# Exponentials and the feed-forward product g split in place in PSUM, a new share-out of the splits among engines, and norms from a matmul with ones

## The chip, the cores and the metric

The kernel runs on one core of a Trainium2 chip. The metric is the device time of one execution in microseconds; lower is better. Times are given in us unless marked ns.

## The reference

Three layers follow each other, all in float32, for B = 2 batches, H = 8 heads, S = 768 tokens of D = 64.

```python
q_n = q / (norm(q) + 1e-6)          # also k_n, c_n
q_assign = argmax(einsum('bhsd,hcd->bhsc', q_n, c_n))   # 16 clusters; k_assign alike
scores = where(q_assign == k_assign, q @ k.T / 8, -1e9)
attn = exp(scores - max(scores)); attn /= sum(attn) + 1e-9
x = (attn @ v)                      # 1536 tokens x 512
h = x @ w_in; g = h * clip(h + 3, 0, 6) / 6; x = g @ w_out           # 512 -> 2048 -> 512
out = sum_e p_e * (relu(x @ w1[e]) @ w2[e])                          # 4 experts, 512 -> 1024 -> 512
```

## The kernel before

**Stages.** For each batch there is an attention, a first feed-forward stage (class Moe1) and a second one (class Moe2). They run in the order attention 0, Moe1(0), Moe2(0) with attention 1 worked in beside it, Moe1(1), Moe2(1). Attention 0 has nothing beside it but the first four of 32 weight tiles to be converted. Moe1(0) carries the other 28 conversions (`conv_w`: float64 bit patterns to float32, four VectorE instructions L770 to L775 a tile, then a split, L749 on ScalarE and L750 on GpSimd). They can start only when the memory of attention 0 is free, since their pools open when its pools close.

**High and low parts.** To keep float32 accuracy each operand is split into a rounded high part and a low remainder, and three matmuls take the place of one (`mm3`, L789 to L791). So each product needs a copy with rounding (the high part, mostly ScalarE) and a subtraction (the low part, VectorE or GpSimd).

**A unit of attention** is 128 queries of one head against all 768 keys; a batch has 48. `scores` puts the score into a tile of two PSUM banks (a ring of three tiles in batch 0, of two in batch 1; a dummy matmul L708 stands ahead in batch 0), VectorE takes the row maximum (L717), ScalarE the exponential with its sum into an SBUF tile e (L718), VectorE scales and inverts the sum (`sums`, L726 and L727). `halves` then makes the two float16 halves p of the probabilities, in one of three ways named by a letter: "P" is GpSimd scaling e in place (L732), ScalarE rounding (L733), GpSimd subtracting (L734); "A" is ScalarE rounding with the scale (L737) and VectorE subtracting (L741); "D" is GpSimd rounding (L739) and VectorE subtracting (L741). In batch 0 the 48 units are 22 P, 13 A and 13 D; in batch 1 they are 12 P and 36 D. A DMA transpose (L673) turns p into pt, matmuls (L686) multiply it with the values, and L694 and L696 split the result.

**Preparation of a pair of heads** (`prep`, four pairs a batch) loads q and k transposed, splits them (L520 to L530, L538), multiplies them with the centroids (L554), transposes these scores (L562), divides them by the norms and makes the one-hot rows of the clusters, which are appended to q and k as rows of the mask. The norms come from a second copy of q and k in natural layout (tensor nat, two loads a pair): `norms` squares it on ScalarE (L495), sums it on VectorE (L496); the root is taken by ScalarE in batch 0 (L505, `roots`) and by GpSimd as a power in batch 1 (L500).

**Moe1** takes its product into a PSUM bank of a ring of three, shared with Moe2 and with the preparation of batch 1. `g1` makes t (L820 on ScalarE, L821 on VectorE, into SBUF), g's high part from t on ScalarE (L822) and its low part on GpSimd (L824) in batch 0, except for every fourth, and on VectorE (L826) otherwise.

**Order.** A class `Order` collects all instructions with what they read and write, and emits them in the order in which a model of the engines would start them; ties go by priorities, planned times that come from the settings `PAR`. Each engine runs its queue in that order.

Of the kernel before, what the change touches and what calls it, by code (L numbers as in the profile page):

```python
# [9 lines left out]
F32 = mybir.dt.float32  # L10
# [10 lines left out]
NEG = 2.0 ** 100  # what a key of another cluster loses; absorbs any score in float32  # L21
PSC = 1024.0  # scale of the probabilities in float16
VSC = 16384.0  # scale of the values in float16, on top of the largest sum over a partition of their head


def _f32(u):
# [3 lines left out]
# Bounds of a float64's high word (seen as float32) whose value float32 can hold.  # L30
# [5 lines left out]
# Settings of the plan: pool depths, the order's look-ahead, priorities in microseconds.  # L36
# [43 lines left out]
class Pool:  # L80
    """A ring of tile slots; opened with its group."""
# [8 lines left out]
class Group:  # L90
    """Pools that open together, once the groups in `after` are closed."""
# [8 lines left out]
class Buf:  # L100
    """A tile that its first writer allocates."""
# [230 lines left out]
def body(ctx: ExitStack, tc: tile.TileContext, qk, nat, vd, cent, w_in, w_out, probs, w1, w2, out):  # L332
# [679 lines left out]
```

## Time and profile before

| | us |
|---|---|
| runs | 1087.26, 1088.27, 1088.45 (median 1088.27) |
| profiled execution, span from first to last instruction | 1088.1 |
| TensorE matmul busy in it | 995.6 (91%) |
| VectorE busy | 634.4 (58%) |
| ScalarE busy | 478.7 (44%) |
| GpSimd busy | 497.8 (46%) |

For the profiled execution nothing but its span is listed; the median of the runs is 0.2 us above that span. A busy share over the whole span says little here, since the stages have different limits; the rows further down are taken by stage. In a row of a group the mean of one instruction stands behind its total, and behind the second bar the time in which its engine sat idle just before such instructions, with what ended it.

### The profile page before, as it was taken

The page shows a single profiled execution, that of the slowest core. Times are in us where ns is not written, and L with a number is a line of the kernel's source. Part 1 is how long each engine was busy: PE and PEld are TensorE (multiplying, and loading weights), DVE is VectorE, ACT ScalarE, POOL GpSimd, SP SyncE. Part 2 cuts the span into 40 slices and gives each one's busy share as a digit, 9 for nine tenths or more (in the row PEclk, how much of TensorE's full clock was granted, in tenths as well). Part 3 has the DMA queues.
Part 4 walks back from the last instruction along what each step waited for, and adds up shares of the span by engine and source line. Part 5 has one row for each costly group of instructions (what it writes and reads, how often), then busy time and mean ns, then how long its engine had stood idle before and what let it go on. Part 6 is the DMA issues. An engine that isn't in the chain of part 4 may idle for free.

```text
span 1088.1 us, 15473 instructions
## 1 busy us (share of the span) xinstructions
PE 995.6 (91%) x5699; PEld 898.5 (83%) x5699; DVE 634.4 (58%) x1103; ACT 478.7 (44%) x893; POOL 497.8 (46%) x385
## 2 busy tenths in 40 slices
PE   3666677988999999999999999999999999999998
PEld 1555556887898888888898898999999899999997
DVE  8999995999536785576476475334453222222222
ACT  6667774545255554345345343444342232222220
POOL 3576864546346776356256164234332333132330
PEclk9678888999999999999999999999999999999999
DMA  8599799676006486367266176222121221112211
GB/s 259 128 201 184 140 187 242 223 245 200 30 2 208 125 168 148 94 134 162 80 145 137 44 156 155 77 78 79 41 67 48 78 78 64 53 50 69 78 39 58
DMA packets 192363, 129.32 MB, mean 119 GB/s; under 512 B 155488, under 2 KB 155488, under 8 KB 192288
## 3 DMA queue, kind: packets, MB, share of 16 engines
q1 hardware_dynamic: 192288, 128.34, 46.1%
q8 instruction: 44, 0.72, 0.3%
q14 instruction: 31, 0.25, 0.1%
HBM read 74.51 MB, written 11.53 MB: 79 GB/s over the span
## 4 chain that ended last, share of the span: by engine, by line
PE 45%; DVE 18%; issue 16%; DMA 9%; POOL 8%; ACT 3%; SPq 1%; POOLq 0%; ACTq 0%; DVEq 0%
PE psm L789 12%; PE psm L791 12%; PE psm L790 12%; DMA pt<-p 6%; POOL w L750 4%; DVE p L741 4%; DVE ut L717 2%; PE psg L790 2%; DVE wconv L773 2%; DVE wconv L770 2%; PE psv L686 2%; PE psg L789 2%; PE psg L791 2%; DVE wconv L775 1%; POOL p L734 1%
## 5 line engine op out<-in xcount | busy, mean ns | idle before, releaser
L750 POOL TENSOR_TENSOR w<-wraw,w 128x512 fp32r<-128x512 f32 x160 | 213.6, 1365 | 289.7 <-ACT w L749 283.6
L864 ACT ACTIVATE h<-psm 128x384 fp32r<-128x384 f32 x128 | 62.4, 488 | 254.9 <-PE psm L791 252.1
L789 PE MATMUL psm<-x2h,w 128*128 128x384 f32 x512 | 173.2, 338 | 0.0
L791 PE MATMUL psm<-x2h,w 128*128 128x384 f32 x512 | 171.8, 336 | 0.0
L790 PE MATMUL psm<-x2l,w 128*128 128x384 f32 x512 | 171.5, 335 | 0.0
L865 DVE SCALAR_TENSOR_TENSOR h<-psm,h 128x384 fp32r<-128x384 f32 x128 | 71.0, 555 | 144.9 <-ACT h L864 144.7
L789 PE MATMUL psm<-w,h 128*128 128x512 f32 x384 | 151.5, 395 | 0.4 <-DVE h L865 0.4
L791 PE MATMUL psm<-w,h 128*128 128x512 f32 x384 | 150.8, 393 | 0.0
L790 PE MATMUL psm<-w,h 128*128 128x512 f32 x384 | 150.4, 392 | 0.0
L880 DVE SCALAR_TENSOR_TENSOR oa<-psm,pr,oa 128x512 f32<-128x512 f32 x84 | 62.8, 748 | 100.8 <-PE psm L791 100.8
L718 ACT ACTIVATE e<-pss,ut 128x768 f32<-128x768 f32 x96 | 86.0, 897 | 72.4 <-DVE ut L717 50.3
L789 PEld LDWEIGHTS psm<-x2h,w 128*128 128x128 f32 x512 | 96.1, 188 | 4.1 <-issue 2.4
L749 ACT ACTIVATE w<-wraw 128x512 fp32r<-128x512 f32 x160 | 93.7, 624 | 11.8 <-PE psm L791 8.1
L741 DVE SCALAR_TENSOR_TENSOR p<-e,ut,p 128x768 f16<-128x768 f32 x62 | 87.6, 1420 | 17.5 <-POOL p L739 15.7
L790 PEld LDWEIGHTS psm<-x2l,w 128*128 128x128 f32 x512 | 96.2, 188 | 1.3
L791 PEld LDWEIGHTS psm<-x2h,w 128*128 128x128 f32 x512 | 96.1, 188 | 0.0
L790 PE MATMUL psg<-g,w 128*128 128x384 f32 x256 | 88.9, 347 | 6.2 <-DVE g L826 4.4
L789 PE MATMUL psg<-x1h,w 128*128 128x384 f32 x256 | 87.3, 341 | 7.7 <-DVE t L821 7.6
L717 DVE TENSOR_REDUCE ut<-pss 128x1 f32<-128x768 f32 x96 | 90.0, 944 | 4.6 <-PE pss L712 4.5
L789 PE MATMUL psg<-g,w 128*128 128x384 f32 x256 | 87.9, 343 | 4.9 <-DVE t L821 4.5
L791 PE MATMUL psg<-g,w 128*128 128x384 f32 x256 | 87.4, 341 | 0.3 <-POOL w L750 0.3
L791 PE MATMUL psg<-x1h,w 128*128 128x384 f32 x256 | 86.7, 339 | 0.0
(125 smaller groups left out, 1913.4 us busy)
## 6 DMA issues: line engine op xcount, KB each, us to landing
wraw<-in_w SPq DMA_DIRECT2D x128, 256.0 KB, 3.2
r<-in_w_in SPq DMA_DIRECT2D x16, 512.0 KB, 5.0
r<-in_w_out SPq DMA_DIRECT2D x16, 512.0 KB, 4.4
nat<-in_nat SPq DMA_DIRECT2D x16, 384.0 KB, 4.4
raw<-in_qk SPq DMA_DIRECT2D x16, 384.0 KB, 4.2
scr_i<-wconv SPq DMA_DIRECT2D x16, 256.0 KB, 2.4
scr_o<-wconv SPq DMA_DIRECT2D x16, 256.0 KB, 3.2
wraw<-scr_i SPq DMA_DIRECT2D x16, 256.0 KB, 2.6
```

What stands on the lines that cost most here:

```text
L686: nc.tensor.matmul(ps[64 * q:64 * q + 64], vs[vi][:, q, t], pts[q][:, :, pi * NT + t], start=i == 0, stop=i == n - 1)
L717: dve(S, p, lambda: nc.vector.tensor_reduce(out=nb(), in_=ps[:, :, 0:HS], axis=AX.XY, op=ALU.max, negate=True), [ps], [(tb, n)])
L718: act(S, p, lambda: nc.scalar.activation(out=e.t.rearrange("p (a b) -> p a b", a=2), in_=ps[:, :, 0:HS], func=AF.Exp, bias=nb(), scale=1.0 ...
L741: dve(S, p, lambda: nc.vector.scalar_tensor_tensor(out=pp[:, j, 1], in0=e.t, scalar=rs(), in1=pp[:, j, 0], op0=ALU.mult, op1=ALU.subtract) ...
L749: act(512, p, lambda: nc.scalar.activation(out=w[:, 0], in_=raw.t, func=AF.Copy), [raw], [(w, 0)])
L750: pool(512, p, lambda: nc.gpsimd.tensor_tensor(out=w[:, 1], in0=raw.t, in1=w[:, 0].bitcast(F32), op=ALU.subtract), [raw, (w, 0)], [(w, 1)])
L789: nc.tensor.matmul(o_, ah, bh, start=i == 0, stop=False)
L790: nc.tensor.matmul(o_, ah, bl, start=False, stop=False)
L791: nc.tensor.matmul(o_, al, bh, start=False, stop=i == 3)
L864: act(MB, p, lambda: nc.scalar.activation(out=h[:, 0], in_=ps[:, 0:MB], func=AF.Relu), [ps], [(h, 0)], ps=True)
L865: dve(MB, p, lambda: nc.vector.scalar_tensor_tensor(out=h[:, 1], in0=ps[:, 0:MB], scalar=0.0, in1=h[:, 0].bitcast(F32), op0=ALU.max, op1=A ...
L880: dve(512, p, lambda: nc.vector.scalar_tensor_tensor(out=oa[:, t], in0=ps.t, scalar=q, in1=oa[:, t], op0=ALU.mult, op1=ALU.add), [ps, pr], ...
```

## The change

The score tile is no longer copied into SBUF: a new letter "M" writes the exponential over the scores in PSUM, and both ScalarE's rounding and VectorE's subtraction read it there. In batch 0 the units become 31 M, 16 P and 1 A, in batch 1 24 D, 12 M and 12 P. In `g1` the product t is written over its PSUM tile, and g's two parts are made from there, the low one always on VectorE. The tensor nat and its loads are gone, with `norms` and `roots`: ScalarE squares the transposed q and k, a matmul with a matrix of ones per head sums them over the 64 rows, and the result goes the way of the centroid scores (copy by ScalarE, three transposes); the root is a power on GpSimd (two instructions of 12 columns a pair), for the first pair of batch 0 a root on ScalarE. The centroid scores leave the ring of score tiles for the ring of single banks (one bank in batch 0). The model in `Order` learns that GpSimd's instructions and VectorE's with two SBUF operands exclude each other (`lock`), and counts 10.8 ns more for a matmul. The settings are other ones; the pool e goes from 6 to 4 tiles, sm from 2 to 3, and the pair order's last two entries are exchanged.

```diff
-    ka=["APDPPDPDADPA", "PADPPAPAAPAP", "PPDPPDDAAPAA", "PDPDPDPDPPAD"],
-    kb="DDDP",
+    ka=["MMPMMPMMPMMP", "MMPMMPMMPMMP", "MMPMMPMMPMMA", "MMPMMPMMPMMP"],
+    kb="DMPD",
...
-                dma(393e3, p, lambda nt=nt, i=i: nc.sync.dma_start(out=nt.t, in_=nat[b, hp, :, 12 * i:12 * i + 12]), [], [nt])
-                act(S, p, lambda nt=nt: nc.scalar.activation(out=nt.t, in_=nt.t, func=AF.Square), [], [nt])
-                dve(S, p, lambda nt=nt, sl=sl: nc.vector.tensor_reduce(out=self.n2[:, sl], in_=nt.t, axis=AX.X, op=ALU.add), [nt], [key])
...
+            for q in range(2):
+                act(S, p(G["sqx"]), lambda q=q: nc.scalar.activation(out=sq[q].t, in_=raws[q].t, func=AF.Square), [raws[q]], [sq[q]])
+            for which in range(2):
+                ps = Buf(p_pm[b], [128, 512], F32, "psc", "prep")
+                def cmm(ps=ps, which=which):
+                    for q in range(2):
+                        lhs, rhs = (ct[:, 2 * hp + q], raws[q]) if which else (bones.t, sq[q])
+                        for f in range(2):
+                            r0 = 64 * f + 32 * q
+                            nc.tensor.matmul(ps[r0:r0 + 32, 0:HS], lhs, rhs[:, f * HS:f * HS + HS], start=True, stop=True)
...
+                act(24, p(4), lambda: nc.scalar.activation(out=fac.t, in_=nsq(), func=AF.Sqrt), [tr[0]], [fac], ps=True, tab=AF.Sqrt)
+            else:
+                dve(24, p(4), lambda: nc.vector.tensor_copy(out=fac.t, in_=nsq()), [tr[0]], [fac])
+                for j in range(2):
+                    pool(12, p(4), lambda js=js: nc.gpsimd.tensor_tensor(out=fac[:, js], in0=fac[:, js], in1=half[:, 0:12], op=ALU.pow), [], [fac], ns=180.0)
...
+            if kind == "M":
+                e, ev = ps, src
+            else:
+                e = self.buf("e", [128, 2, HS], F32)
...
-                if kind == "A":
+                if kind in "AM":
...
-            dve(MB, p, lambda: nc.vector.scalar_tensor_tensor(out=t.t, in0=t.t, scalar=1.0, in1=ps[:, 0:MB], op0=ALU.min, op1=ALU.mult), [ps], [t])
-            act(MB, p, lambda: nc.scalar.activation(out=g[:, 0], in_=t.t, func=AF.Copy), [t], [(g, 0)])
-            if b == 0 and f != 3:
-                pool(MB, p, lambda: nc.gpsimd.tensor_tensor(out=g[:, 1], in0=t.t, in1=g[:, 0].bitcast(F32), op=ALU.subtract), [t, (g, 0)], [(g, 1)])
+            dve(MB, p, lambda: nc.vector.scalar_tensor_tensor(out=ps[:, 0:MB], in0=t.t, scalar=1.0, in1=ps[:, 0:MB], op0=ALU.min, op1=ALU.mult), [t], [ps])
+            act(MB, p, lambda: nc.scalar.activation(out=g[:, 0], in_=ps[:, 0:MB], func=AF.Copy), [ps], [(g, 0)], ps=True)
+            dve(MB, p, lambda: nc.vector.tensor_tensor(out=g[:, 1], in0=ps[:, 0:MB], in1=g[:, 0].bitcast(F32), op=ALU.subtract), [ps, (g, 0)], [(g, 1)])
```

## Rows read from the trace of the kernel before

**Rows 1.** By stretch: length, busy PE, PEld, DVE, ACT, POOL; TensorE clock, DMA share, GB/s

```profile
0.00:30.00 30.00, 12.76 (x62) 7.21 (x62) 26.61 (x65) 20.89 (x31) 10.17 (x13) 1.00 0.80 260
30.00:120.00 90.00, 58.57 (x388) 46.19 (x389) 88.97 (x166) 65.09 (x119) 65.99 (x47) 0.77 0.81 161
120.00:172.00 52.00, 38.32 (x312) 31.19 (x307) 43.31 (x87) 34.41 (x66) 33.89 (x25) 0.84 0.94 171
172.00:285.00 113.00, 96.32 (x510) 89.07 (x508) 100.19 (x151) 52.27 (x97) 54.95 (x37) 0.92 0.67 214
285.00:700.00 415.00, 407.31 (x2428) 367.93 (x2428) 247.27 (x437) 190.11 (x363) 217.94 (x176) 1.00 0.50 120
700.00:1088.10 388.10, 382.31 (x2012) 356.90 (x2011) 128.04 (x198) 115.97 (x219) 114.88 (x88) 1.00 0.20 62
```

**Rows 2.** Groups by line, VectorE in 0 to 172 us (attention 0)

```profile
L717 DVE TENSOR_REDUCE ut<-pss 128x1 f32<-128x768 f32 x48 | 44.9, 941 | 0.9 <-PE pss L712 0.8
...
L741 DVE SCALAR_TENSOR_TENSOR p<-e,ut,p 128x768 f16<-128x768 f32 x25 | 38.9, 1567 | 2.1 <-ACT p L737 1.7 <-POOL p L739 0.4
...
L526 DVE SCALAR_TENSOR_TENSOR qa<-raw,qa 64x768 fp32r<-64x768 f32 x8 | 11.3, 1416 | 0.3
...
L496 DVE TENSOR_REDUCE n<-nat 128x12 f32<-128x768 f32 x8 | 7.5, 945 | 0.2
```

**Rows 3.** The same view, GpSimd, ScalarE and TensorE in 0 to 172 us

```profile
L718 ACT ACTIVATE e<-pss,ut 128x768 f32<-128x768 f32 x48 | 42.8, 893 | 18.5 <-DVE ut L717 15.8 <-DVE sv L641 2.0 <-DVE ut L726 0.5
...
L734 POOL TENSOR_TENSOR p<-e,p 128x768 f16<-128x768 f32 x22 | 39.9, 1820 | 6.6 <-ACT p L733 6.3
...
L732 POOL TENSOR_SCALAR e<-e,ut 128x768 f32<-128x768 f32 x22 | 24.5, 1114 | 23.7 <-DVE ut L726 9.9 <-ACT e L718 5.9 <-DVE ut L727 4.0
...
L708 PE MATMUL pss<-junk,ident_b 128*128 128x384 bf16 x48 | 19.5, 407 | 33.4 <-ACT e L718 33.4
...
L739 POOL TENSOR_SCALAR p<-e,ut 128x768 f16<-128x768 f32 x12 | 12.1, 1011 | 3.1 <-DMA pt<-p 1.6 <-issue 1.1 <-DVE tv L633 0.2
L737 ACT ACTIVATE p<-e,ut 128x768 f16<-128x768 f32 x13 | 12.1, 932 | 4.4 <-DMA pt<-p 3.0 <-DVE ut L727 1.1 <-ACT e L718 0.2
```

**Rows 4.** Timeline, 54 to 58 us: start, duration, engine, line

```profile
54.58 1.95 POOL L734 TENSOR_TENSOR p<-e,p 128x768 f16<-128x768 f32 x1
54.96 2.38 DVE L741 SCALAR_TENSOR_TENSOR p<-e,ut,p 128x768 f16<-128x768 f32 x1
```

**Rows 5.** All instructions of line 865: ns minimum, median, maximum, times

```profile
L865 DVE SCALAR_TENSOR_TENSOR h<-psm,h x128: 532/558/558, 334.3 to 1076.5; 128x384 fp32r<-128x384 f32 x128
```

**Rows 6.** Groups by line, VectorE and GpSimd in 172 to 285 us (Moe1 of batch 0)

```profile
L750 POOL TENSOR_TENSOR w<-wconv,w 128x512 fp32r<-128x512 f32 x20 | 34.7, 1753 | 13.1 <-ACT w L749 9.0 <-issue 4.1
...
L775 DVE SCALAR_TENSOR_TENSOR wconv<-r,wconv 128x512 int32<-128x512 int32 x28 | 24.9, 890 | 0.2
L773 DVE SCALAR_TENSOR_TENSOR wconv<-r,wconv 128x512 int32<-128x512 int32 x28 | 23.6, 842 | 0.2
L824 POOL TENSOR_TENSOR g<-t,g 128x384 fp32r<-128x384 f32 x16 | 19.9, 1241 | 38.4 <-ACT g L822 29.5 <-PE psg L791 8.9
L770 DVE TENSOR_SCALAR wconv<-wconv 128x512 f32<-128x512 f32 x28 | 19.0, 680 | 1.8 <-ACT wconv L769 1.8
...
L826 DVE TENSOR_TENSOR g<-t,g 128x384 fp32r<-128x384 f32 x5 | 4.9, 980 | 0.6 <-ACT g L822 0.6
```

**Rows 7.** All instructions of line 770

```profile
L770 DVE TENSOR_SCALAR wconv<-wconv x32: 412/420/1515, 20.2 to 273.8; 128x512 f32<-128x512 f32 x32
```

**Rows 8.** All instructions of line 773

```profile
L773 DVE SCALAR_TENSOR_TENSOR wconv<-r,wconv x32: 677/684/1664, 48.9 to 278.0; 128x512 int32<-128x512 int32 x32
```

**Rows 9.** Groups by line, 331 to 700 us (Moe2 of batch 0 beside attention 1)

```profile
L500 POOL TENSOR_TENSOR n<-n,half 128x6 f32<-128x6 f32 x16 | 24.3, 1524 | 11.5 <-DVE n L496 7.4 <-DVE n L570 2.0 <-DVE ut L726 1.3
...
L554 PE MATMUL psc<-raw,ct 128*32 128x384 f32 x32 | 3.4, 498 | 0.0
...
L562 PE MATMUL psct<-ident,sc 128*128 128x128 f32 x12 | 2.0, 272 | 0.0
```

More of the change, by code (lines that the diff above doesn't have):

```diff
@@ L143, in group, with add @@
         return g
-    def add(self, eng, dur, prio, fn, reads=(), writes=(), dma=0.0, cols=0, tab=None):
+    def add(self, eng, dur, prio, fn, reads=(), writes=(), dma=0.0, cols=0, tab=None, lock=False):
         t = Task()
+        t.lock = lock or eng == "POOL"
         t.cols, t.tab = cols, tab
@@ L244, in plan @@
                     s = t.ready if t.ready > fe else fe
+                    if t.lock and port > s:
+                        s = port
                     ok = True
@@ L295, in plan @@
                 free[t.eng] = end
+                if t.lock:
+                    port = end
             t.end = end
@@ L331, in body @@
 @with_exitstack
-def body(ctx: ExitStack, tc: tile.TileContext, qk, nat, vd, cent, w_in, w_out, probs, w1, w2, out):
+def body(ctx: ExitStack, tc: tile.TileContext, qk, vd, cent, w_in, w_out, probs, w1, w2, out):
     nc = tc.nc
@@ L424, in body @@
     ct = fixed([128, H, 32], F32, "ct")
+    bones = fixed([128, 32], F32, "bones")
     cn = fixed([128, D], F32, "cn")
@@ new lines, in prep, with ctr @@
+            tr = []
+            for which in range(2):
[6 more added lines that the diff above has]
+                            nc.tensor.matmul(ps[r0:r0 + 32, 0:HS], lhs, rhs[:, f * HS:f * HS + HS], start=True, stop=True)
+                px = p(G["psx"] + 0.5 * which)
+                pe(0.7, px, cmm, [*raws, ct] if which else [*sq, bones], [ps], 4 * HS)
+                sc = self.buf("sc", [128, HS], F32)
+                act(HS, px, lambda sc=sc, ps=ps: nc.scalar.activation(out=sc.t, in_=ps[:, 0:HS], func=AF.Copy), [ps], [sc], ps=True)
+                ps = Buf(p_pm[b], [128, 512], F32, "psct", "prep")
+                def ctr(ps=ps, sc=sc):
+                    for i in range(3):
+                        nc.tensor.transpose(ps[:, i * 128:i * 128 + 128], sc[:, i * 128:(i + 1) * 128], ident.t)
+                pe(0.33, p(G["psx"] + 0.3 + 0.5 * which), ctr, [sc], [ps])
+                tr.append(ps)
@@ L663, in block @@
                     tb = self.buf("tiny", [128, 8], F32, "ut")
-                    es = [self.scores(qa, qb, ka, kb, blk * BQ + (j0 + n) * 128, tb, n, p(q * JQ + j0 + n)) for n in range(step)]
+                    es = [self.scores(qa, qb, ka, kb, blk * BQ + (j0 + n) * 128, tb, n, p(q * JQ + j0 + n), kinds[(q * JQ + j0 + n) % len(kinds)]) for n in range(step)]
                     self.sums(tb, step, p(q * JQ + j0))
@@ L893, in body @@
     centroids(-50.0)
-    for hp in range(NP):
-        a0.norms(hp, G["nat0"] if hp == 0 else 4.0 + 0.5 * hp, 0)
-    a0.roots(0, 1, -49.7)
-    a0.roots(1, NP, G["nroot"])
     when = {(x // NBQ, x % NBQ): T_A + i * 2 * JQ * T_UNIT for i, x in enumerate(G["seq"])}
```

165 lines of the change are left out of this document (68 added, 97 removed).

## The prediction

> **What bounds the kernel now.** I read the busy times by stretch first [rows 1]. They show three regimes. From 285 us on TensorE has work all the time: it is busy for 407.3 of 415 us up to 700 and for 382.3 of 388.1 after that, at full clock. Whatever moves work among the other engines there can win at most the 13.5 us that are left, and work added to TensorE lengthens the run. From 0 to 172 us (attention 0) VectorE is busy for 26.6 + 89.0 + 43.3 = 158.9 us, in the middle stretch for 89.0 of 90, while TensorE, ScalarE and GpSimd have room (TensorE 58.6, ScalarE 65.1, GpSimd 66.0 of 90). From 172 to 285 us (Moe1 of batch 0 with the weight conversions) VectorE is busy again, for 100.2 of 113 us, and TensorE loses 16.7 us there. So VectorE sets the first 285 us, and what is saved on it there brings the long TensorE part forward.
>
> Second, I read the groups by line of attention 0, to see what VectorE's time is made of [rows 2]. L741, the low part of p, takes 1567 ns on average, while the reduction of as many columns L717 takes 941. The timeline shows why [rows 4]: L741 starts at 54.96 while GpSimd's subtraction L734 runs from 54.58 to 56.53, and ends at 57.34, 0.81 us after GpSimd is done. Two operands in SBUF make VectorE wait for a running GpSimd instruction, and that time counts as busy. An instruction with one operand in PSUM does not show it: L865 runs 128 times beside GpSimd's weight splits and never takes more than 558 ns [rows 5].
>
> **The change part by part.** The sum is made against the span of 1088.1 us; the median of the runs lies 0.2 us above it.
>
> *Norms, batch 0.* The eight sums L496 go: 8 x 945 ns = 7.5 us off VectorE [rows 2]. All of them are in the stretch that VectorE bounds, so they count in full. What comes for them on VectorE is three copies of 24 columns, under half a us together. GpSimd gets six roots of 12 columns. A root of 6 columns takes 1524 ns in batch 1 [rows 9]; one of 12 costs between that and twice that, six between 9 and 18 us, and I take 13.5. ScalarE squares as often as before. The matmul with ones and its transposes lie in a stretch where TensorE has a third of its time free [rows 1].
>
> *Probabilities, batch 0.* The 25 L741 of this stretch cost 38.9 us [rows 2]. After it there are 31 of kind M and one of kind A. For M, which reads PSUM, the bound from below is the reduction L717 from PSUM over the same 768 columns, 0.94 us, that from above twice L865, which has half the columns, 1.12 us [rows 2, 5]. I take 1.0: 31 x 1.0 + 1.57 = 32.6 us, a gain of 6.3 us (8.2 and 2.6 at the bounds).
>
> The Trainium skill speaks against this: its page VectorE: DVE Perf Modes, section "The TRN2 errata — SBUF-src ops pay a fixed extra latency per instruction", gives VectorE a fixed 120 cycles for a source in PSUM and 58 for one in SBUF. By it each M would take 62 cycles more, an estimated 65 ns at that page's 0.96 GHz, 2.0 us in all, and the result would be 1078. The trace doesn't show such a price: the reduction of 768 columns takes 941 ns from PSUM (L717) and 945 from SBUF (L496) [rows 2].
>
> *GpSimd, batch 0.* A unit of kind P costs it 1.114 + 1.820 = 2.93 us, one of kind D 1.01 [rows 3]. 22 P and 12 D make 76.5 us, 16 P make 46.9; with the roots GpSimd falls from 110 us in this stretch to 94, by 15%. VectorE's other instructions with two SBUF operands are blocked less: L526 alone runs 8 x (1.416 - 0.945) = 3.8 us over the one-operand time [rows 2]. The gain lies between 0 and that 3.8 as a whole; I take 2, since L526 is not the only one.
>
> *ScalarE, batch 0.* Roundings go from 35 (22 P, 13 A) to 48, so 13 x 0.93 = 12 us more, on 120 us before [rows 1, 3]. In some 158 us that is 84%: hidden beside VectorE. The exponential now writes PSUM, for which no row has a price; it reads PSUM already at 893 ns [rows 3], and the rounding from SBUF takes 932, so I take no difference, and up to 0.04 x 31 = 1.2 us either way on an engine with room.
>
> *The ring of score tiles.* An M unit keeps its tile through the rounding (0.93 us) and the low part (1.0), at least 1.9 us longer. 31 units make 59 us, over three tiles 20 us. From below it is nothing, if TensorE runs that far ahead: it sits idle for 33.4 us before L708 until an exponential has freed a tile [rows 3], and VectorE's queue, not the tile, is what these tiles are waiting in. VectorE would need about 145 us for 48 units, 3.0 a unit, and three tiles give each unit 9 us, so I take 2 us of the 20.
>
> Attention 0: -7.5 - 6.3 - 2 + 2 = -13.8 us.
>
> *Moe1, batch 0.* The 28 conversions in 172 to 285 us are blocked by GpSimd: L770 takes 680 ns against a median of 420, L773 842 against 684, L775 890 [rows 6 to 8]. With L771 taken like L770 and L775's floor like L773's, that is 28 x (2 x 0.26 + 0.158 + 0.206) = 24.8 us. L824 is 19.9 of GpSimd's 55.0 us there and goes; 36% of the blocking is 9.0 us. Against it VectorE gets these 16 subtractions, at L865's 0.558 us [rows 5], 8.9 us, and the five L826 fall from 0.980 to 0.558, -2.1 us. Net -2.2 us, between +6.8 (nothing relieved) and -18 (all of it).
>
> *Batch 1.* TensorE gets a second set of L554 and L562, 3.4 + 2.0 = 5.4 us at most [rows 9], in a stretch where it has 7.7 of 415 us free [rows 1]. Some of it falls into such a gap; I take +4 (0 to 5.4). Twelve units M for D and the missing L496 relieve VectorE, which sets nothing there (247 of 415 us); the missing loads of nat relieve the DMA queue, whose share is 0.50. In the last stage g's parts come from PSUM beside a VectorE at a third of its time: 0.
>
> Sum: 1088.1 - 13.8 - 2.2 + 4 = 1076.1, as a median 1076.
>
> **The rivals.** *The blocking goes altogether.* With M at its lower bound (-1.9), no price for the score tiles (-2), L526 at its floor (-1.8) and no blocking in the conversions (-15.8) it is 1054.6. For it: the blocking is a matter of who runs beside whom, and of GpSimd's subtractions six of 22 L734 leave and all L824 [rows 3, 6]. Against: the weight splits L750 stay, and they are 34.7 of its 55 us in Moe1 [rows 6]. Chance 0.18.
>
> *The transposes set attention 0.* The DMA share is 0.81 from 30 to 120 us and 0.94 after that [rows 1], 122 us of work in 142. If it can't be packed closer, only the 7.5 us of L496, most of which come ahead of the first transpose, are won there: 1088.1 - 7.5 - 2.2 + 4 = 1082.4. For it: 0.94 in the last stretch. Against: L739 and L737 wait only 1.6 and 3.0 us for a transpose [rows 3]. Chance 0.14.
>
> *The score tiles set attention 0: slower.* If all three tiles are booked all the time, the 20 us appear in full in place of the 2: 1076.1 + 18 = 1094. It decides from 16 us on; below that the run is still no slower than before by more than 0.2%. For it: the 33.4 us in which TensorE already waits for a free tile [rows 3], and each M passes VectorE three times. Against: VectorE's 89 of 90 us, which make that wait back-pressure. The Trainium skill's page ScalarE: Activation LUTs, section "Step-by-step: what each stage is for", recommends PSUM as ScalarE's destination only where TensorE does not need most of it; it does here, and that caveat is this rival. No run so far shows which holds. Chance 0.12.
>
> *The product banks set Moe1: no change.* g's rounding and subtraction keep a bank at least 2 x 0.56 us longer. 32 such tiles over a ring of three make 12 us, if the banks are booked all the time, and with 5.4 instead of 4 us in batch 1 it is 1089. For it: TensorE loses 16.7 us in that stretch, VectorE's queue is full and is now passed twice. Against: twelve matmuls fill a bank, and 510 of them take 113 us there [rows 1], so that a bank is needed every 2.7 us and three give each 8. Chance 0.10.
>
> **How the numbers follow.** The forecast has 0.46; its own range is 1066 to 1086. Faster by over 0.2% (2.2 us, about what a measurement of this kernel can tell from no change) is nearly all of it (0.45), the first rival (0.18), 0.13 of the second and 0.01 of the last: 0.77. Within 0.2% lie 0.05 of the last rival and 0.01 each of forecast and second: 0.07. Slower: the third (0.12) and 0.04 of the last: 0.16. The range from 1054 to 1094 leaves out half of the first and of the third rival, 0.15.
>
> **What the profile would show.** Right: the mean of L741's successors with a PSUM operand at 1.0 us, all within 0.1; VectorE still over 90% busy until attention 0 ends, and that end, now about 172, near 158; the first product of Moe1 as much earlier; the conversions' four lines shorter in sum by some 9 us; TensorE at full clock from then on with 4 us more of small matmuls in batch 1. Wrong: VectorE idle between units while TensorE waits for a tile (the score ring), a DMA share near 1 with waits for p's tiles (the transposes), TensorE waiting for the low part of g (the banks), or an M split that takes as long as before.

## The result, and the profile after

The kernel after takes 1097.37 us (median of 4 runs, 1096.75 to 1101.66) against 1088.35 for the kernel before beside it: ratio 1.0084, 95% interval 1.0061 to 1.0108. It is slower by 0.8%, where the prediction said 1076 and faster. The profiled execution is the one of 1101.66 us, some 4 us above the other three; its span is 1099.9. One count given with the change is wrong: its settings make 32 M, 15 P and 1 A of batch 0's 48 units, not 31, 16 and 1. The splits of one M and of the A come after 172 us.

The busy times by stretch, as in [rows 1], of the kernel after:

```profile
0.00:30.00 30.00, 15.56 (x85) 7.85 (x85) 24.82 (x75) 23.28 (x40) 12.12 (x15) 1.00 0.57 179
30.00:120.00 90.00, 61.17 (x398) 44.23 (x399) 69.67 (x144) 65.74 (x113) 51.31 (x36) 0.75 0.81 156
120.00:172.00 52.00, 38.17 (x275) 29.70 (x273) 45.26 (x104) 39.82 (x75) 18.56 (x14) 0.84 0.84 158
172.00:285.00 113.00, 101.91 (x595) 98.82 (x596) 92.82 (x163) 57.68 (x108) 29.60 (x22) 0.95 0.69 211
285.00:700.00 415.00, 400.70 (x2340) 345.48 (x2340) 243.81 (x440) 193.46 (x362) 187.83 (x145) 0.99 0.46 112
```

VectorE did lose its work: 24.82 + 69.67 + 45.26 = 139.8 us up to 172 us, 19.1 less than before [rows 1]. But attention 0 is not shorter. VectorE is now busy for 69.67 of the 90 us in the middle, where it was busy for 89; the time saved turned into idle time.

To see where the span went I cut each trace at four events: the first score matmul, the first product of Moe1(0), the first of Moe2(0), and the point where 55% of the recorded products are done, which is after attention 1. Between them lie these times in us, for all later kernels too; each ratio is to runs of the kernel before made beside that kernel. The medians are of all runs, the stretches of the one profiled execution:

| kernel | median | ratio, 95% | start | attention 0 | Moe1(0) | Moe2(0) with attention 1 | rest |
|---|---|---|---|---|---|---|---|
| before | 1088.4 | | 25.9 | 139.5 | 166.1 | 388.4 | 368.2 |
| after | 1097.4 | 1.0084 [1.0061, 1.0108] | 23.9 | 142.7 | 156.6 | 410.8 | 365.8 |
| e1 | 1090.4 | 1.0016 [0.9998, 1.0034] | 23.5 | 141.6 | 156.4 | 401.1 | 365.8 |
| e2 | 1113.8 | 1.0235 [1.0213, 1.0257] | 23.7 | 154.0 | 160.0 | 407.3 | 365.8 |
| e3 | 1103.6 | 1.0131 [1.0108, 1.0155] | 23.9 | 151.9 | 158.2 | 402.1 | 365.8 |
| e4 | 1086.9 | 0.9976 [0.9965, 0.9988] | 26.3 | 136.8 | 165.4 | 389.5 | 365.9 |
| e5 | 1097.5 | 1.0080 [1.0051, 1.0109] | 28.6 | 144.5 | 162.5 | 392.0 | 365.9 |
| e6 | 1108.3 | 1.0168 [1.0144, 1.0192] | 22.6 | 154.1 | 160.7 | 402.5 | 368.2 |
| e7 | 1107.2 | 1.0162 [1.0144, 1.0180] | 29.0 | 141.8 | 166.9 | 397.4 | 368.2 |
| e8 | 1095.1 | 1.0056 [1.0032, 1.0081] | 26.3 | 147.7 | 165.5 | 387.9 | 365.9 |
| e9 | 1092.0 | 1.0023 [1.0008, 1.0038] | 24.9 | 139.4 | 168.8 | 387.9 | 368.3 |
| e10 | 1093.0 | 1.0040 [1.0028, 1.0052] | 24.7 | 138.8 | 167.6 | 390.4 | 368.2 |
| e11 | 1097.8 | 1.0079 [1.0054, 1.0103] | 26.5 | 139.6 | 164.8 | 397.8 | 368.2 |
| e12 | 1089.6 | 1.0008 [0.9996, 1.0019] | 24.1 | 141.0 | 155.9 | 400.7 | 365.8 |
| e13 | 1102.1 | 1.0118 [1.0096, 1.0141] | 28.4 | 145.2 | 169.9 | 389.0 | 368.2 |
| e14 | 1122.2 | 1.0313 [1.0274, 1.0351] | 25.6 | 161.9 | 158.9 | 410.2 | 365.8 |
| e15 | 1088.4 | 0.9986 [0.9971, 1.0001] | 24.2 | 142.8 | 153.0 | 401.9 | 365.8 |
| e16 | 1108.5 | 1.0178 [1.0155, 1.0202] | 27.1 | 153.4 | 168.8 | 390.4 | 368.2 |
| e17 | 1081.3 | 0.9940 [0.9918, 0.9961] | 23.3 | 142.3 | 155.4 | 393.1 | 365.8 |
| e18 | 1101.9 | 1.0127 [1.0101, 1.0154] | 24.1 | 154.5 | 161.8 | 393.4 | 365.8 |

So before to after: start -2.0, attention 0 +3.2, Moe1(0) -9.5, Moe2(0) with attention 1 +22.4, rest -2.4. Together that is 11.7 us, where the medians differ by 9.0: some 3 us of it belong to the two executions and not to the kernels. Two places call for a reason: attention 0, which should have got 13.8 us shorter, and Moe2 with attention 1, which should have got 4 us longer.

The chain of work that ended last, share of the span by engine, in the kernel before and in the kernel after:

```profile
PE 45%; DVE 18%; issue 16%; DMA 9%; POOL 8%; ACT 3%; SPq 1%; POOLq 0%; ACTq 0%; DVEq 0%
```

```profile
PE 58%; DMA 11%; issue 7%; DVE 7%; ACT 5%; POOL 4%; SPq 1%; ACTq 0%; POOLq 0%; DVEq 0%
```

"issue" is time in which the engine waited for nothing that the profile shows. The shares of VectorE, GpSimd and issue fell; what they gave up went to TensorE and, less, to DMAs and ScalarE.

**Attention 0.** The line numbers have moved: L724 is L717 of before, L749 L741, L725 L718, L710 L708, L513 L526; L570 are the new roots. The groups of 0 to 172 us that answer to [rows 2, 3], VectorE, ScalarE, TensorE, GpSimd:

```profile
L724 DVE TENSOR_REDUCE ut<-pss 128x1 f32<-128x768 f32 x48 | 44.7, 949 | 11.5 <-PE pss L714 11.3
...
L749 DVE SCALAR_TENSOR_TENSOR p<-pss,ut,p 128x768 f16<-128x768 f32 x31 | 31.2, 1014 | 7.5 <-ACT p L745 7.0 <-issue 0.2
...
L725 ACT ACTIVATE pss<-pss,ut 128x768 f32<-128x768 f32 x32 | 27.8, 868 | 10.6 <-DVE ut L724 10.2 <-DVE ut L732 0.3
...
L710 PE MATMUL pss<-junk,ident_b 128*128 128x384 bf16 x48 | 18.5, 384 | 21.8 <-DVE p L749 15.1 <-ACT e L725 3.2 <-DVE ut L732 2.0
...
L725 ACT ACTIVATE e<-pss,ut 128x768 f32<-128x768 f32 x16 | 14.3, 897 | 2.6 <-DVE ut L724 2.6
L570 POOL TENSOR_TENSOR fac<-fac,half 128x12 f32<-128x12 f32 x6 | 14.1, 2351 | 9.7 <-DVE fac L567 9.6
...
L513 DVE SCALAR_TENSOR_TENSOR qa<-raw,qa 64x768 fp32r<-64x768 f32 x8 | 9.7, 1224 | 0.6 <-ACT qa L507 0.5
```

VectorE now waits 11.3 us for scores and 7.0 for ScalarE's rounding (L745), where it waited 0.8 for scores before [rows 2]. TensorE's wait ahead of a score has another releaser: 33.4 us for an exponential before [rows 3], now 15.1 for the low part L749 of an M unit, which gives the tile back. One such wait in the order of TensorE's queue, from the timeline of 94 to 102 us (start, duration, wait in brackets):

```profile
95.91 0.34 PE L710 MATMUL pss<-junk,ident_b 128*128 128x384 bf16 x1
...
96.88 0.85 PE L547 MATMUL psc<-sq,bones 128*32 128x384 f32 x8
101.44 0.34 PE L710 MATMUL pss<-junk,ident_b 128*128 128x384 bf16 x1 [3.70 <-DVE p L749]
```

From one score to the next pass 5.5 us, 3.70 of them idle. But in all TensorE waits less for tiles than before (21.8 us ahead of L710 in the row above, 33.4 in [rows 3]), and it waits somewhat more for transposes. The largest waits for either in 26 to 165 us (total, times, longest), first before, then after:

```profile
PE pss L708 <- ACT e L718: 33.4, 20, 5.0
PE psv L686 <- DMA pt<-p: 4.2, 2, 2.6
```

```profile
PE pss L710 <- DVE p L749: 15.1, 9, 3.7
PE psv L688 <- DMA pt<-p: 6.7, 5, 2.7
```

The price of the M split itself is what was predicted; the 31 that fall ahead of 172 us (minimum, median, maximum):

```profile
L749 DVE SCALAR_TENSOR_TENSOR p<-pss,ut,p x31: 1007/1017/1019, 31.0 to 170.6; 128x768 f16<-128x768 f32 x31
```

**Moe2 with attention 1.** The waits of TensorE there, 323 to 712 us (total, times, longest):

```profile
PE pss L712 <- ACT e L725: 8.4, 6, 2.0
PE psv L688 <- DMA pt<-p: 3.4, 4, 1.1
PE psm L797 <- ACT h L869: 1.3, 1, 1.3
```

The first row is waits for a score tile. In the kernel before, the same view of 323 to 712 us has none; its longest entry is

```profile
PE psv L686 <- DMA pt<-p: 6.2, 7, 1.9
```

The granted clock is below 1.00 in two places of the stretch. One lies behind a wait for a score tile (1.93 us, ending at 477), the other behind a wait of a product of Moe2 for its h (L797, ending at 339). By stretch:

```profile
330.00:340.00 10.00, 8.65 (x45) 7.47 (x43) 4.90 (x6) 6.89 (x11) 4.97 (x4) 1.00 0.78 243
340.00:350.00 10.00, 9.71 (x40) 6.78 (x41) 6.05 (x15) 2.35 (x7) 0.25 (x1) 0.83 0.03 5
350.00:360.00 10.00, 10.00 (x60) 8.60 (x60) 4.15 (x8) 4.79 (x9) 7.53 (x5) 1.00 0.40 131
...
470.00:480.00 10.00, 8.07 (x37) 7.04 (x36) 5.83 (x10) 3.59 (x7) 2.51 (x2) 0.88 0.37 80
480.00:490.00 10.00, 8.95 (x63) 6.46 (x62) 6.47 (x11) 4.53 (x8) 2.59 (x3) 0.95 0.52 115
...
650.00:660.00 10.00, 8.03 (x46) 7.71 (x45) 5.94 (x14) 6.31 (x13) 7.30 (x6) 1.00 0.64 169
660.00:670.00 10.00, 10.00 (x74) 8.11 (x73) 6.81 (x13) 5.39 (x10) 3.47 (x3) 1.00 0.70 158
```

In either place a part was at 1.2 GHz and not at 2.4; by the granted clock that is 1.7 us of work each, some 3.4 of the 22.4. The other five waits for a tile have no lower clock behind them, as the rows of 650 to 670 us show for the longest (1.97 us).

### The profile page after: what moved, and what is told of

Its sections match the earlier page's. It is cut to its first block, busy times and chain, and to the rows that moved or that the text cites. A ratio compares the mean times of both kernels' runs of the same rounds, so it can differ in the third digit from the quotient of the medians.

```text
span 1099.9 us, 15658 instructions
## 1 busy us (share of the span) xinstructions
PE 1013.4 (92%) x5787; PEld 898.2 (82%) x5787; DVE 600.9 (55%) x1128; ACT 501.2 (46%) x925; POOL 414.0 (38%) x320
## 4 chain that ended last, share of the span: by engine, by line
PE 58%; DMA 11%; issue 7%; DVE 7%; ACT 5%; POOL 4%; SPq 1%; ACTq 0%; POOLq 0%; DVEq 0%
PE psm L797 13%; PE psm L799 13%; PE psm L798 13%; DMA pt<-p 7%; PE psg L797 5%; PE psg L798 5%; PE psg L799 5%; PE psv L688 2%; DVE p L749 2%; DMA r<-in_w_out 2%; DMA r<-in_w_in 1%; POOL w L758 1%; POOL p L742 1%; DVE ut L724 1%; PE pss L712 1%
## 5 line engine op out<-in xcount | busy, mean ns | idle before, releaser
L758 POOL TENSOR_TENSOR w<-wraw,w 128x512 fp32r<-128x512 f32 x160 | 207.9, 1330 | 316.7 <-ACT w L757 313.7
L797 PE MATMUL psm<-x2h,w 128*128 128x384 f32 x512 | 174.5, 341 | 0.0
L797 PE MATMUL psm<-w,h 128*128 128x512 f32 x384 | 153.0, 398 | 1.3 <-ACT h L869 1.3
L797 PEld LDWEIGHTS psm<-x2h,w 128*128 128x128 f32 x512 | 96.1, 188 | 7.0 <-issue 3.0
L724 DVE TENSOR_REDUCE ut<-pss 128x1 f32<-128x768 f32 x96 | 89.6, 951 | 21.8 <-PE pss L714 21.2
L797 PE MATMUL psg<-x1h,w 128*128 128x384 f32 x256 | 87.0, 340 | 4.0 <-DVE g L831 4.0
L797 PE MATMUL psg<-g,w 128*128 128x384 f32 x256 | 86.6, 338 | 4.0 <-DVE g L831 4.0
L797 PEld LDWEIGHTS psm<-w,h 128*128 128x128 f32 x384 | 72.9, 190 | 19.0 <-issue 3.3
L799 PEld LDWEIGHTS psm<-w,h 128*128 128x128 f32 x384 | 72.8, 190 | 17.2 <-DVE h L870 1.6
L798 PE MATMUL psg<-g,w 128*128 128x384 f32 x256 | 86.3, 337 | 0.2 <-DVE g L831 0.2
L798 PE MATMUL psg<-x1l,w 128*128 128x384 f32 x256 | 86.3, 337 | 0.0
```

The lines of the kernel that those rows point to most:

```text
L724: dve(S, p, lambda: nc.vector.tensor_reduce(out=nb(), in_=src(), axis=AX.XY, op=ALU.max, negate=True), [ps], [(tb, n)])
L758: pool(512, p, lambda: nc.gpsimd.tensor_tensor(out=w[:, 1], in0=raw.t, in1=w[:, 0].bitcast(F32), op=ALU.subtract), [raw, (w, 0)], [(w, 1)])
L797: nc.tensor.matmul(o_, ah, bh, start=i == 0, stop=False)
L798: nc.tensor.matmul(o_, ah, bl, start=False, stop=False)
L799: nc.tensor.matmul(o_, al, bh, start=False, stop=i == 3)
```

## The experiments

### M in either batch: e1, e2, e3

The kernel after with the kinds of before in batch 1, in batch 0, in both; everything else is the kernel after.

```diff
-    ka=["MMPMMPMMPMMP", "MMPMMPMMPMMP", "MMPMMPMMPMMA", "MMPMMPMMPMMP"],
-    kb="DMPD",
+    ka=["APDPPDPDADPA", "PADPPAPAAPAP", "PPDPPDDAAPAA", "PDPDPDPDPPAD"],   # e2, e3
+    kb="DDDP",                                                             # e1, e3
```

> The changed kernel with batch 1's units as before the change (36 D, 12 P, none M). Tile theory: an M unit keeps one of batch 1's two score tiles through its splits, TensorE's queue stands at the next score, and the product matmuls stand behind it; without M the stretch of Moe2 of batch 0 gets the 5.5 us of added gaps back and the 3 us of half clock that follow them, so 1097 - 8 = 1089. Order theory: the new settings and the new order model place attention 1 badly, whatever the letters; 1094 to 1100.

> The changed kernel with batch 0's units as before the change (22 P, 13 A, 13 D, none M). Tile theory: the ring of three score tiles set attention 0; with the exponential back in SBUF VectorE is the bound again, over 95% busy, less the 7.5 us of L496, and the first Moe1 product comes at some 158 to 160 instead of 166: 1097 - 7 = 1090. Order theory: the letters don't matter or cost VectorE its blocked time again, first product at 166 or later, 1097 to 1103.

> The changed kernel with the units of both batches as before the change. Tile theory: both gains together, 1097 - 15 = 1082, faster than before the change, since what is left is the norms' matmul and g in PSUM. Order theory: 1095 to 1103.

Without M in batch 1 the run is 7.0 us shorter (1097.4 to 1090.4) and Moe2 with attention 1 goes from 410.8 to 401.1; with no M in batch 0 either it is 10.3 (e2 to e3). So in this order M in batch 1 costs. But most of TensorE's waits for a score tile stay without it; e1, 321 to 712 us:

```profile
PE pss L712 <- ACT e L725: 5.7, 5, 2.6
```

M in batch 0 gains: e3 to e1 is -13.2 us, attention 0 151.9 to 141.6. e2 and e3 were slower than either of their theories said, so M in batch 0 is not what made attention 0 longer under this order. The change's worth in attention 0 is real beside the rest of the new kernel, but what it is added to is 12 us longer than before.

### The order against the work: e4, e5, e6, e16

e4 is the kernel before with g in PSUM alone, e5 the kernel after (its M in both batches, its norms, g and pools) with the old settings and the old model in `Order`, e6 the kernel before with the new ones, e16 the kernel before with the new model alone.

```diff
-            dve(MB, p, lambda: nc.vector.scalar_tensor_tensor(out=t.t, in0=t.t, scalar=1.0, in1=ps[:, 0:MB], op0=ALU.min, op1=ALU.mult), [ps], [t])
+            dve(MB, p, lambda: nc.vector.scalar_tensor_tensor(out=ps[:, 0:MB], in0=t.t, scalar=1.0, in1=ps[:, 0:MB], op0=ALU.min, op1=ALU.mult), [t], [ps])   # e4, and both parts of g from ps
-    mm = lambda n: 1e-3 * (n / 2.4 + 2.5)
+    mm = lambda n: 1e-3 * (n / 2.4 + 13.3)   # e6 and e16, with the lock; e5 the reverse
-    slack=0.05,
+    slack=0.15425516062141928,               # e6, with all settings of the order; e5 the reverse
```

> The kernel before the change with g alone made in PSUM and its low part always on VectorE. If the gain in Moe1 of batch 0 (8 to 13 us in the changed kernel's trace) comes from g, this kernel is at 1076 to 1081. If it comes from the new order, it is at 1085 to 1091.

> The changed kernel with the order of before: the old settings (priorities, look-ahead, pair order) and the old model in Order (no lock, matmuls 10.8 ns shorter); kinds, g, norms and pools as changed. If the new order is what cost attention 0 its 10 us (first Moe1 product at 176 without M, against 165), this is at 1084 to 1088 and its first product at 156 or so. If the norms' longer chain or the M letters cost it, it stays at 1094 to 1100.

> The kernel before the change with the new settings and the new model alone (kinds, g and norms as before). If the new order costs, 1089 + 10 to 15 = 1099 to 1104; if the norms cost, 1086 to 1091.

> The kernel before with the planner's new model of durations (each matmul 11 ns more, and the lock between VectorE and GpSimd), old settings. The whole new order, model and settings, cost 19 us on the old work. If the model is at fault: 8 to 20 us slower than before. If the settings are: within 4 us of before, as the two small changes of the order were.

g in PSUM is a gain by itself: 0.24%, with 2.3 us of it in the last stage (368.2 to 365.9), where I had put nothing. The blocking of the conversions fell as expected; VectorE's conversions in 172 to 285 us of e4, which answer to [rows 6]:

```profile
L775 DVE SCALAR_TENSOR_TENSOR wconv<-r,wconv 128x512 int32<-128x512 int32 x28 | 23.6, 842 | 0.2
L773 DVE SCALAR_TENSOR_TENSOR wconv<-r,wconv 128x512 int32<-128x512 int32 x28 | 21.9, 783 | 0.2
...
L770 DVE TENSOR_SCALAR wconv<-wconv 128x512 f32<-128x512 f32 x28 | 16.3, 587 | 6.8 <-ACT wconv L769 6.7
L771 DVE TENSOR_SCALAR wconv<-wconv 128x512 int32<-128x512 int32 x28 | 13.9, 495 | 0.2
```

They take 75.7 us together against 24.9 + 23.6 + 19.0 + 17.9 = 85.4, 9.7 less; predicted were 9.0.

The new order on the old work costs 1.68% (18 us, e6), and the model alone 1.78% (e16): attention 0 goes from 139.5 to 153.4 with the same instructions. The 30 to 120 us of e16:

```profile
30.00:120.00 90.00, 61.11 (x364) 47.20 (x362) 79.94 (x153) 60.92 (x109) 57.71 (x40) 0.70 0.75 158
```

VectorE is busy for 79.94 of 90 us there and attention 0 is 14 us longer: that it was busy for 89 before [rows 1] was the work of one order, not the amount of the work. The granted clock is 0.70 there, 0.77 before; what that adds no run separates. The new settings take 8 us off Moe1(0) (168.8 to 160.7) and put 12 on Moe2 with attention 1 (390.4 to 402.5), with no M in it. e6 is beyond the range that its text gave to the order, and e5 in the one that it gave to the norms and the kinds: in attention 0 either costs. On the new work neither order is better as a whole (e5 and after), but they lose in other places: 392.0 against 410.8 in Moe2 with attention 1, 162.5 against 156.6 in Moe1(0).

e5 and e6 also tell whose the waits for score tiles in Moe2 with attention 1 are. e6 has none of the M and 5.7 us of them (337 to 740 us); e5 has the twelve M, and no such wait (336 to 728 us, the longest entry shown):

```profile
PE pss L715 <- ACT e L723: 5.7, 7, 1.4
```

```profile
PE psc L547 <- DVE h L870: 3.2, 1, 3.2
```

So these waits come with the new settings, not with the M.

### Single edits in the old order: e7, e8

e7 is the kernel before with the new norms and what the change does for them (the centroid scores in the single banks, 4 tiles e in place of 6, 3 of sm), e8 is e4 with the kinds of the change in batch 0, 32 M.

```diff
-    ka=["APDPPDPDADPA", "PADPPAPAAPAP", "PPDPPDDAAPAA", "PDPDPDPDPPAD"],
+    ka=["MMPMMPMMPMMP", "MMPMMPMMPMMP", "MMPMMPMMPMMA", "MMPMMPMMPMMP"],   # e8, on e4
...
-                dve(S, p, lambda nt=nt, sl=sl: nc.vector.tensor_reduce(out=self.n2[:, sl], in_=nt.t, axis=AX.X, op=ALU.add), [nt], [key])
+                        lhs, rhs = (ct[:, 2 * hp + q], raws[q]) if which else (bones.t, sq[q])   # e7
```

> The kernel before the change with the norms by a matmul with ones alone (old kinds, old g, old order). By the prediction's terms, 7.5 us off VectorE in attention 0 and 4 us more on TensorE in batch 1: 1085. If the longer chain of the norms (square, matmul, copy, transposes, copy, root on GpSimd) or the one bank they share holds up the units, 1097 to 1103.

> The kernel before the change with g in PSUM and with batch 0's units as changed (31 M, 16 P, 1 A), batch 1's units, norms and order as before. M in batch 0 was worth 13 us (1103.6 without, 1090.4 with) in the changed kernel: if that holds here, 1087 - 13 = 1074. If M pays only where VectorE is not the bound of the order, 1080 to 1090.

In the old order the norms cost 1.62% (17.6 us), where the prediction's terms made a gain of 3.5 of them; by the stages of the profiled executions 3.1 at the start, 2.3 in attention 0, 9.0 in Moe2 with attention 1. What the smaller pool e has in it isn't separated. In batch 0 M costs 8.2 over e4, where under the new order it gained 13; e8 is slower than either of its theories said. In 30 to 120 us of e8:

```profile
30.00:120.00 90.00, 59.66 (x358) 45.50 (x357) 75.29 (x164) 67.69 (x117) 41.20 (x32) 0.70 0.77 158
```

VectorE and GpSimd both have less to do than in e4 and attention 0 is 10.9 us longer (136.8 to 147.7). TensorE waits less for tiles there than in e4, and much more for transposes (16.5 us against 2.9); e8, 26 to 165 us:

```profile
PE psv L686 <- DMA pt<-p: 16.5, 8, 3.8
PE pss L708 <- ACT e L723: 11.0, 7, 4.1
PE pss L708 <- DVE p L747: 7.0, 6, 2.0
```

### How much any other order costs: e9, e10, e11

The kernel before with one setting changed (e9, e10) or with the five new settings of batch 1 (e11); the instructions are the same.

```diff
-    slack=0.05,
+    slack=0.06,                     # e9
-    lead0=24.98317741027136,
+    lead0=23.98317741027136,        # e10
-    btail=10.347963191960837,
+    btail=15.313072883537151,       # e11, with bu0, bdu, bvl and bpr of the change
```

> The kernel before the change with one setting moved, slack from 0.05 to 0.06: the same instructions, in another order on every engine. Fit theory (the order of before is fitted to its mix of instructions, and any other order of much the same quality costs 10 to 19 us, so that each edit alone pays that first): 1097 to 1105, with attention 0 longer by 5 to 12 us. Work theory (each edit's own cost made the losses of the runs so far, and orders of one model are worth about the same): 1086 to 1092.

> The kernel before the change with lead0 lower by 1 us: preparation of the pairs planned 1 us later, the same instructions in another order. Fit theory: 1095 to 1105. Work theory: 1086 to 1092.

> The kernel before the change with the changed kernel's five settings of attention 1 (btail, bu0, bdu, bvl, bpr) alone. If these place attention 1 badly beside Moe2 of batch 0, that stretch grows from 388 by the 12 to 14 us that the whole new order cost there: 1101 to 1104. If the loss there comes from the new model or the other settings, 1087 to 1093.

The two small changes of the order cost 2.5 and 4.4 us, less than the fit theory said. So a changed order can cost a few us by itself, and a term of that size can't be told from it; the 18 us of the new order are more. The five settings cost 8.6 us, between the two theories; 9.4 are in the stretch that they plan, and with them come waits for score tiles, though e11 has no M (321 to 712 us):

```profile
PE pss L710 <- ACT e L718: 6.4, 8, 2.0
```

### The score tiles: e13, e14

Two score tiles in batch 0 in place of three, in the kernel before and in the kernel after.

```diff
-    p_s = [Pool("ps_sa", 3, g_pa, True), Pool("ps_sb", 2, g_ps, True)]
+    p_s = [Pool("ps_sa", 2, g_pa, True), Pool("ps_sb", 2, g_ps, True)]
```

> The kernel before with two score tiles in place of three in batch 0 (the planner knows it and lays its order accordingly). In the kernel before a score tile is given back when its exponential is done, some 5.4 us after its fill; 48 x 5.4 / 2 = 130 us, which still fits into the 139 us of attention 0. Theory of the score tiles: attention 0 becomes 0 to 15 us longer. Rival (every change of the order costs as such, whatever resource it takes): about the same loss as in the kernel after with two tiles.

> The kernel after with two score tiles in place of three in batch 0. An M unit holds its tile for 8.8 us on average, a P unit for 5.4: (31 x 8.8 + 17 x 5.4) / 2 = 182 us. Theory (with M the score tiles set attention 0): it grows from 143 to 165 to 185 us, the whole run by 20 to 40. Rival (VectorE sets attention 0 and the wait for tiles is back-pressure): under 10 us more. Rival (order as such): as much as the kernel before with two tiles.

Attention 0 gets 5.7 us longer in the kernel before and 19.2 in the kernel after, short of the 165 expected; the whole run 13.2 and 24.8. One number of the expectation was wrong: a tile of the kernel before is held for 7.3 us on average, not 5.4. I took the mean of 48 holds, from the k-th dummy matmul to the k-th exponential, or to the low part for an M. By that, the tiles are booked for 48 x 7.30 / 3 = 117 of 139.5 us before (84%), and 48 x 7.71 / 3 = 123 of 142.7 after (86%; 8.84 for an M, 5.44 for the others). With two tiles the hold shrinks to 4.84 in the kernel before (80% of 145.2), but only to 6.39 in the kernel after (95% of 161.9). So in the kernel before a third of a tile's time was waiting that could be spared (back-pressure, as I had said), in the kernel after a sixth; an M there still holds its tile for 7.55 us, another unit for 4.07. The tiles count for more after the change: with two, they nearly fill attention 0. With three that is not shown. By the hold of e14 they would need 48 x 6.39 / 3 = 102 of the 142.7 us.

TensorE's waits in 26 to 165 us of e14, where the first row was 15.1 us with three tiles:

```profile
PE pss L710 <- DVE p L749: 24.5, 10, 5.2
PE psv L688 <- DMA pt<-p: 11.0, 5, 4.0
PE pss L710 <- ACT e L725: 7.6, 6, 1.8
```

### Moe2 with attention 1, and fewer M in batch 0: e12, e15, e17, e18

All have `kb="DDDP"`. e12 has the old five settings of batch 1, e15 the old planned time of the AV products in batch 1, e17 both; e18 is e17 with 16 M and 32 P in batch 0.

```diff
-    btail=15.313072883537151,
+    btail=10.347963191960837,       # e12, e17, e18, with bu0, bdu, bvl and bpr of before
-                    a1.block(hp, blk, lambda i, u0=u0, du=du, blk=blk: u0 + (4 * blk + i) * du, G["kb"], G["xbb"], G["avp"])
+                    a1.block(hp, blk, lambda i, u0=u0, du=du, blk=blk: u0 + (4 * blk + i) * du, G["kb"], G["xbb"], -9.142989452549473)   # e15, e17, e18
+    ka=["MPPMPPMPPMPP"] * 4,        # e18
```

> The changed kernel without M in batch 1 and with the old five settings of attention 1. Moe1 of batch 0 keeps its 10 us, attention 0 its length; if the five settings made the other 12 us of loss beside Moe2, this is at 1090 - 10 = 1080, faster than both kernels. If not, 1087 to 1095.

> The kernel after without M in batch 1, and with the old planned time (avp) of the product of p and v in batch 1 alone; batch 0 keeps the new one. Theory: the new avp puts these matmuls one by one among the products of Moe2, and the switching costs the 10 to 12 us by which the stretch of Moe2 and attention 1 is still longer than before (401 against 388): it falls to 388 to 392 and the run to 1076 to 1081. Rival: the loss lies in other settings or in the second set of small matmuls, and the run stays at 1087 to 1092.

> The kernel after without M in batch 1, and with both the five settings of batch 1 and the planned time of its AV products of before. Either of the two alone left Moe2 with attention 1 at 401 to 402 us: with one of them the switches between kinds of matmul stayed at 190 to 203, with the other they fell to 154 but TensorE waited 12 us. Theory (the two settings fit only each other): both together give 386 to 393 us and the run 1073 to 1081, the fastest here. Rival (the loss is the second set of small matmuls and the new model): the stretch stays at 398 to 403 and the run at 1086 to 1091.

> As the run before it, with 16 units M and 32 P in batch 0 instead of 31 M, 16 P, 1 A. Theory (the score tile is what an M costs): the mean hold falls from 7.6 to 6.5 us, the tiles leave more room, and attention 0 is shorter than with 31 M by 2 to 10 us. Rival (GpSimd and what it blocks on VectorE set attention 0): 16 P more at 2.93 us each put GpSimd from about 94 to over 130 us, and attention 0 is longer by 5 to 15 us.

Each of the two alone leaves the stretch at 401 to 402 us, as the rivals had it. e15 still has 5.5 us of waits for score tiles. e12 has none, and TensorE idle for as long as in e17 (8 us); but its matmuls switch between the kinds of tile that they write 203 times in the stretch, against 169, and the stretch is 7.6 us longer. Both settings together bring it to 393.1 and the run to 1081.3, which no other kernel here reaches: 0.6% below before, 1.5% below after (1081.3 / 1097.4). The median missed the expected range by 0.3 us, the stretch the upper end by 0.1. TensorE's waits there, 323 to 712 us of e17, have no score tile left; the longest is now the norms' matmul, which waits for VectorE's h of Moe2:

```profile
PE psc L547 <- DVE h L870: 3.8, 1, 3.8
PE psv L688 <- DMA pt<-p: 2.1, 2, 1.5
```

That is no shorter than e5 with its twelve M (392.0); e17 with M in batch 1 was not run. What remains above before is 4.7 us; the second set of small matmuls, which was put at 4, is in every kernel with the new norms. Its groups in the kernel after, 323 to 712 us (12 more transposes and 32 more matmuls than in [rows 9]):

```profile
L557 PE MATMUL psct<-ident,sc 128*128 128x128 f32 x24 | 3.9, 271 | 0.0
L547 PE MATMUL psc<-sq,bones 128*32 128x384 f32 x32 | 3.4, 498 | 0.0
L547 PE MATMUL psc<-raw,ct 128*32 128x384 f32 x32 | 3.4, 498 | 0.0
```

e18 went against the tiles as the only price: with half as many M attention 0 is 12.2 us longer, as the rival had it, though the tiles are booked for only 48 x 7.50 / 3 = 120 of 154.5 us (78%). The hold fell from 7.71 us only to that 7.50, not to 6.5. In its 30 to 120 us GpSimd is busy for 74.22 and VectorE for less than in e17:

```profile
30.00:120.00 90.00, 58.73 (x376) 43.09 (x376) 67.38 (x137) 64.12 (x112) 74.22 (x50) 0.76 0.77 155
```

No engine is full, but each P goes through GpSimd twice. Why a GpSimd that is busy for 82% costs that much isn't shown by a run.

## Why the prediction was wrong

**What failed first is the premise.** "So VectorE sets the first 285 us, and what is saved on it there brings the long TensorE part forward." The saving came, and more of it (19.1 us against 7.5 + 6.3 + 2 = 15.8), but attention 0 did not get shorter by it. VectorE's 89 of 90 us showed that under this one order VectorE was the last to be waited for. Other orders with the same work (e6, e16), or the old settings with less work for VectorE (e7, e8), make attention 0 longer while VectorE has 10 to 15 of the 90 us free. A unit goes from TensorE to VectorE, ScalarE, ScalarE or GpSimd, VectorE and a transpose before TensorE gets it back, through queues in fixed order and three tiles. In the kernel after VectorE was idle for 20.3 of the 90 us. What attention 0 ends on in its place stays open.

**"All of them are in the stretch that VectorE bounds, so they count in full"**, the -7.5 of the norms, failed with it: in the old order the norms made start and attention 0 5.4 us longer (e7). Under the new order no run tests them.

**"I take 2 us of the 20"** for the ring of score tiles is a term that no run sizes. I held that TensorE's 33.4 us of waiting were back-pressure. For the kernel before that is right (e13: the hold shrinks from 7.3 to 4.8 us when a tile is taken). But I drew from it that a longer hold costs next to nothing, and after the change less of the hold can be spared (e14: 6.4 us, and 19.2 us in attention 0 for a tile, against 5.7). How much of the 13.8 + 1.2 = 15.0 us that fail in start and attention 0 together is the tiles, how much the norms and how much the new model's order, the runs don't separate: taking M away makes it worse under this order (e3, e18), so the tiles are not all of it, and the 33.4 us of waits fell to 21.8.

The rival with the score tiles had 1094, near the 1097.4, and its 18 us in attention 0 are near these 15.0. That is in part luck: e3 and e18 speak against the tiles as the whole cause there, and it had neither the 18.4 us by which Moe2 with attention 1 missed its +4, nor the 9.7 us by which Moe1(0) and the last stage came out better.

**"Twelve units M for D ... relieve VectorE, which sets nothing there"** is the failed step in batch 1, together with its new settings, on which the prediction spent no word and which the sum so has at nothing. Five of the settings alone put 9.4 us on that stretch (e11), all of them 12.1 (e16 to e6); the old five and the old time of the AV products give 8.0 back (e1 to e17). They bring the waits for score tiles, 5.7 to 6.4 us with no M in that batch (e1, e6, e11). On top of them the M add 2.7 us of such waits (8.4) and cost 7.0 us of median (e1). Under the old settings the twelve M have no such wait and the stretch is 392.0 (e5). So the step missed that TensorE, the engine without room, is the one that waits there, and that the plan of the batch decides whether a longer hold is felt.

The Trainium skill's page ScalarE: Activation LUTs, section "Step-by-step: what each stage is for", has PSUM as ScalarE's destination useful only if TensorE doesn't need most of it. The trace agrees in part: the exponential itself became 29 ns shorter (868 against 897 ns), and in batch 1 the tile was missed under the new settings, but not under the old ones.

**"I take +4 (0 to 5.4)"** for the second set of small matmuls fits what is left in e17, 4.7; in e7, the norms without the rest, the stretch grew by 9.0, so the fit may hold some luck.

**Moe1(0)** was better than said, -9.5 against -2.2. g alone gives -0.7 there in the old order (e4), near the -2.2; the new order alone -5.4 (e6). **The last stage**, put at 0, gave -2.4, nearly all from g (e4: -2.3).

**The single prices held.** M 1.014 us for 1.0; the six roots 14.1 us for 13.5; L513 1224 ns, 1.5 us less in eight, of the 2 I gave to the lesser blocking; no blocking of an M, which reads PSUM (1019 ns at most). With the miscounted unit the term of the probabilities is 32 x 1.0 + 1.57 = 33.6 and not 32.6, 1 us of the sum; GpSimd, put at 94 us, was busy for 12.12 + 51.31 + 18.56 = 82.0. By the Trainium skill's page VectorE: DVE Perf Modes, section "The TRN2 errata — SBUF-src ops pay a fixed extra latency per instruction", an M would have been an estimated 65 ns longer than the same split from SBUF. The trace doesn't agree: the 25 splits from SBUF of the kernel after (the A and the D units) have the same minimum and median, 1007 and 1017 ns:

```profile
L749 DVE SCALAR_TENSOR_TENSOR p<-e,ut,p x25: 1007/1017/2386, 175.2 to 681.7; 128x768 f16<-128x768 f32 x25
```

Of the other rivals, that the blocking goes altogether and that the product banks set Moe1 did not come: Moe1(0) is shorter, by less than 18 us. The transposes stand untested. The DMA share of attention 0 did not rise (0.81 and 0.84), but in the chain of 26 to 165 us the rows DMA pt<-p went from 2.9% to 10.9%, and in e8 TensorE waits 16.5 us for them; no run gives them less to do.

## What to carry to other kernels

An engine that is busy all the time in one stage shows that this order of the queues ends there, not that the stage shrinks with its work: ask how many units the buffers hold in flight and how long each is held, and multiply (units x hold / buffers) against the stage, before and after. A measured hold has waiting in it; a run with one buffer less shows how much of it can be spared. Where a change keeps a PSUM tile longer, price it in each stage by who waits for that tile, and under the order in which it will run: the same twelve M cost 7 us under one plan and showed no price under another. Settings of an order are part of the work that they were fitted to; when work moves, test each part with its own, and each stage by itself: the best kernel here is the change without M in batch 1 and with the old plan of that batch.

## What was not expected of the hardware

A wait of TensorE has no fixed price. A wait of 1.34 us, ending at 339 us, was followed by a granted clock of 0.83 over the stretch of 340 to 350 us, in which it was busy for 9.71 us; at that clock these 10 us hold 1.7 us less work, more than the wait itself. Waits of 1.80 and 1.97 us, ending at 386 and 653 us, were followed by 1.00, as was one of 1.88 us at 480 us of the kernel before. What makes the difference isn't shown.

A GpSimd power of 12 columns takes 2351 ns where one of 6 took 1524 [rows 9]: 1.54 times as long for twice the columns.
